# Gated mix of attention and a channel MLP: weight pieces split, statistics and first maxima moved, the tail's sums loaded in parts

## The chip, the cores and the metric

The kernel runs on one core of a Trainium2 chip. Five engines of the core matter here: TensorE (PE in the profile) multiplies matrices and writes PSUM banks of 128 x 512 float32, VectorE (DVE), ScalarE (ACT) and GpSimd (POOL) work elementwise, and SyncE (SP) issues most of the DMA transfers. Each engine takes its instructions in the order in which they were written and stands still at one whose semaphores are not there yet. The metric is the device time of one execution in microseconds, the median of three runs; the profile is of one more execution.

## The reference

The input x has 2048 tokens of width 576. What is computed:

```
g = sigmoid((x * gate_w).sum(-1, keepdims=True))
a = softmax_attention(x @ wqkv, 32 heads of 18) @ wo        # scale 18 ** -0.5
y = (x - mean(x)) / sqrt(var(x) + 1e-5)
b = gelu_tanh(y @ w1 + b1) @ w2 + b2                          # 576 -> 4608 -> 576
out = g * a + (1 - g) * b
```

Everything is float32. The kernel gets that precision out of TensorE by cutting each factor into a high part (a rounded copy, written by ScalarE) and a low part (the factor minus that copy, written by VectorE or GpSimd), and adding three products.

## The kernel before, in words

The work has three stages, and the order within each engine's queue is the order in which the Python code writes the instructions.

**Stage 1, the projections (to about 224 us of the span).** Four blocks `tb` of 512 tokens. For each block TensorE runs 17 groups `g` of 14 matmuls: nine `qk_group` (128 rows of Q and K, 512 tokens wide; L881 to L884) and eight `v_group` (128 tokens, 288 columns of V; L902 to L905), in PSUM banks of a pool of four, `ps_a`. Behind each group the code may hang other work, by tables at the head of the file:

- `W_AT`: before which groups of block 0 a piece of the QKV weights is cut into high and low (`split_w`, L751 on ScalarE, L752 on VectorE or GpSimd). The seven pieces arrive by DMA into two buffers of the pool `pp`, so a piece's load waits for the piece two before it. The bounds of the pieces are `W_CUT`.
- `N_AT`: behind which groups of block 0 its layer norm is worked out. `norm` has four stages: 0 and 1 take the statistics of two of the block's four groups of 128 tokens each (L844, L845) and stage 1 ends with the reciprocal deviation (L850 to L857); 2 and 3 take the gate's sum (L867) and, in block 0, write the normed tokens over x (L870). The gate's product goes to a scratch tile of the pool `pp`, too.
- `BLOCK[tb]`: the same for block `tb + 1`, whose x is loaded ahead (`load`). `stats` is the group behind which its statistics begin (stage 0, and stage 1 a group later), `rows` the group behind which they are transposed and stored (`stat_rows`, L826 to L828), `wide` the group behind which they are read back as rows spread over all partitions (`load_wide`, L832, into `wide`, which is the tile `qa` in the profile), `gate` the group behind which the gate's sums come, `x` the first of five groups behind which x is transposed (`x_chunk`, L757). `x_chunk` writes, from one bank: x minus the mean (L772, VectorE, needs `wide`), the high part (L774, ScalarE) and the low part (L775, VectorE). In block 0 `y_chunk` does the same with the normed tokens behind groups 12 to 16 (L757, L805, L806).
- `ROUNDS[tb](g)`: how many rounds of first maxima follow group `g`. A round is two score matmuls (L227) and two maxima over 512 scores on VectorE (L229, 128 x 512 to 128 x 1); its results give the softmax its first row maxima. Forty rounds must be done before stage 2.

**Stage 2, the loop (to about 2190 us).** 512 steps of attention, into which the MLP's matmuls are dealt out as filler, and in the last steps those of the tail's first blocks. The change does not touch its order.

**Stage 3, the tail.** `out_proj` runs four blocks `b` of 512 tokens. A block has eight groups of 14 matmuls (L1205), two for each 128 tokens; behind each, VectorE forms the result from the bank, the gate and the MLP's sums `BT[b][t]` (L1209). The banks are a pool of two, so a group waits for the result two groups before it. Between these results VectorE and ScalarE prepare the next block's factor: `normed(b, stage)` multiplies a 128 x 512 piece of the unscaled attention output `o` by the reciprocal sums `den` (L1122) and cuts it (L1125, L1132); `PLAN` sets behind which group which stage stands. The last unit of attention ends while block 1 is under way; then `over` loads what had to wait for it. `load_rest(b)` loads the last unit's rows of `o` and `den` (L1093, L1098), and `last_loads` the MLP sums of block 2 (`load_b`, L1104, tile `bt`), and `o` and `den` of block 3 (L1056, L1059, L1078, L1081). `load_den` calls `load_rest` at its end once the last unit is over.

DMA transfers take turns on eight completion counters, over all queues: an issue waits until the transfer eight places before it in the program has landed. SP's queue stands still for as long, with all that is behind it.

Of the kernel before, what the change touches and what calls it, by code (L numbers as in the profile page):

```python
# [8 lines left out]
F32 = mybir.dt.float32  # L9
F32R = mybir.dt.float32r  # L10
AF = mybir.ActivationFunctionType
ALU = mybir.AluOpType
# [4 lines left out]
P = 128  # L17
# [7 lines left out]
TB = 512  # L25
# [25 lines left out]
LAST = 28  # L51
PSTEP = (489, 492, 495, 497)
ORDER = (0, 1, 3, 2)
ROUNDS = [lambda g: 0, lambda g: 2 * (g in (9, 11, 13, 15)), lambda g: 2 * (g % 2 and g != 17),
          lambda g: 2 * (g in (4, 5, 6, 7, 8, 10, 12, 14))]
SLOTS = [lambda g: 0, lambda g: 0, lambda g: int(g >= 4), lambda g: 1 if g < 9 else 2]
SKIP = 0
N_AT = {3: (0, ()), 4: (1, ()), 7: (2, (0,)), 8: (3, (1,)), 9: (3, (2,)), 10: (3, (3,))}
BLOCK = [dict(stats=0, rows=4, wide=5, x=11, lag=4, gate=16, load=16),
         dict(stats=5, rows=8, wide=9, x=11, lag=3, gate=7, load=13),  # L60
         dict(stats=0, rows=3, wide=4, x=6, lag=3, gate=3)]
W_AT = {0: 1, 1: 2, 2: 3, 4: 4, 6: 5, 7: 6}
W_CUT = (0, 128, 416, 704, 992, 2 * D, 3 * D - 288, 3 * D)
# [5 lines left out]
def gated_mix_kernel(ctx: ExitStack, tc: tile.TileContext, x, wqkv, wo, w1, b1, w2, b2, gate_w, out):  # L69
    nc = tc.nc  # L70
    x = x[0]
# [15 lines left out]
    b_scr = dram.tile([S, D], F32, name="b_scr")  # L87
# [617 lines left out]
    with ExitStack() as a:  # L705
# [41 lines left out]
        def split_w(n, eng):  # L747
            c0 = W_CUT[n] if W_CUT[n] < 2 * D else W_CUT[n] - 2 * D
            hi, lo = [w_[:, :, c0:c0 + W_CUT[n + 1] - W_CUT[n]] for w_ in (W_QK if W_CUT[n] < 2 * D else W_V)]
            raw = wraw.pop(n)  # L750
            nc.scalar.activation(hi, raw, AF.Copy)  # L751
            eng.tensor_tensor(lo, raw, hi.bitcast(F32), op=ALU.subtract)  # L752

        def transposed(tb, c):
            ps = psum(ps_a)
# [182 lines left out]
        for tb in range(NB):  # L938
            work = [(qk_group, (tb, mt)) for mt in (range(9) if tb < 2 else (4, 0, 1, 2, 3, 5, 6, 7, 8))] + [(v_group, (tb, t, n)) for t in range(4) for n in range(2)]
            for g, (fn, args) in enumerate(work):  # L940
                if tb == 0:
                    if g in W_AT:
                        n = W_AT[g]
# [82 lines left out]
    def out_proj():  # L1026
# [36 lines left out]
        def load_den(b):  # L1063

            while len(stored) < (NU - 2 if b < 2 else NU - 1):
                run_due()
            if b == 0:
                wide = low.bitcast(F32)[:, 0:4, :]
                den = [low.bitcast(F32)[:, c, :] for c in range(5)]
            elif b % 2 == 0:  # L1070
                wide = KA[0].bitcast(F32).rearrange("p (c n) -> p c n", c=4)
                den = [wide[:, c, :] for c in range(4)] + [QA[2][:, :TB].bitcast(F32)]
            else:
                tile_ = io.tile([P, 5, TB], F32, name="den", bufs=1)
                wide = tile_[:, 0:4, :]
                den = [tile_[:, c, :] for c in range(5)]
            cols = slice(b * TB, (b + 1) * TB)
            nc.sync.dma_start(wide, ot_scr[1, 0:512, cols].rearrange("(c p) n -> p c n", p=P))  # L1078
            for h in range(2):
                e = 64 if b < 2 else LAST  # L1080
                nc.sync.dma_start(den[4][64 * h:64 * h + e], ot_scr[1, 512:512 + e, cols])  # L1081
            OT[b].append(den)
            if ended[0]:
                load_rest(b)

        ready = {0, 1}

# [10 lines left out]
                    nc.sync.dma_start(den[4][r:r + DH], sums[j:j + 1, :].to_broadcast([DH, TB]))  # L1098
            ready.add(b)

        def load_b(b):
            t0 = len(BT.setdefault(b, []))
            bt = io.tile([P, 4 - t0, D], F32, name="bt", bufs=2)
            nc.sync.dma_start(bt, b_scr[b * TB + t0 * P:(b + 1) * TB, :].rearrange("(t p) d -> p t d", p=P))  # L1104
            BT[b] += [bt[:, t] for t in range(4 - t0)]

        def load_b_first():
            BT[0] = [QA[0].bitcast(F32)[:, :D], VT[0].rearrange("p k e -> p (k e)")[:, :D]]
# [40 lines left out]
        held = []  # L1149

        def last_loads():
            load_b(2)
            load_o(3)
            load_den(3)
        waiting = []

        def go_on(last):
# [20 lines left out]
        io = ctx.enter_context(tc.tile_pool(name="c_io", bufs=3))  # L1178
        load_o(1)
        load_den(1)  # L1180
        load_b(0)
        yield 0
        for b in range(NB):
            if b == 1 and not ended[0]:
                held.append(last_loads)
            elif b == 1:
                last_loads()
            elif b + 1 < NB:
                load_b(b + 1)
            for t in range(4):  # L1190
                if b == 0 and t == 1:
                    load_o(2)
# [127 lines left out]
```

## Time and profile before

| | us |
| --- | --- |
| median of 3 runs | 2240.97 (2240.55 to 2241.92) |
| the profiled execution's own time | 2240.88 |
| its span | 2239.1 |
| TensorE busy | 2216.3 |
| VectorE busy | 1644.1 |
| ScalarE busy | 1427.3 |
| GpSimd busy | 1002.9 |

The profile counts time from the start of the span. A row of its timeline has the start, the time from the first start to the last end of the instructions merged in it, the engine, the line, the operation, what is written and read, the count, and in brackets the idle time before it and what ended it. A letter q behind an engine's name is its queue: there the time is that of issuing. A row of the waits has a sum, a count and the longest. Times of matmuls overlap, so the distance from one row's start to the next is what a stretch of matmuls takes.

### The profile page before, as it was taken

What the parts mean: (1) busy time and instruction counts of PE and PEld (TensorE: products, weight loads), DVE (VectorE), ACT (ScalarE), POOL (GpSimd) and SP (SyncE); (2) the same over time, 40 slices, a digit from 0 to 9 for tenths busy, and PEclk for the clock granted to TensorE, in tenths of its full rate; (3) what the DMA queues carried; (4) which work ended last, traced back from release to release, by engine and by line L of the source; (5) the groups of instructions that cost most, each with busy time, mean ns of one, the idle gap of its engine ahead of it and who ended that gap; (6) DMA issues with size and microseconds to landing.
All of it is one profiled execution on the core that took longest, in us unless ns stands there. A gap on an engine that the chain in (4) does not pass through costs nothing.

```text
span 2239.1 us, 51576 instructions
## 1 busy us (share of the span) xinstructions
PE 2216.3 (99%) x20528; PEld 1578.7 (71%) x20528; DVE 1644.1 (73%) x2886; ACT 1427.3 (64%) x2653; POOL 1002.9 (45%) x1001
## 2 busy tenths in 40 slices
PE   8999999999999999999999999999999999999999
PEld 7878666766767677667677667677676676676668
DVE  5685677777778777777777777777777777777734
ACT  4233677777767666666666666666666666666772
POOL 3241666666655444444454444444444444444710
PEclk9999999999999999999999999999999999999999
DMA  8767654445455524333354424233364323242264
GB/s 252 240 210 245 213 174 131 145 157 170 133 198 159 173 87 155 103 128 114 109 156 154 132 87 144 100 119 103 117 179 144 107 100 120 103 148 89 92 221 167
DMA packets 164104, 329.23 MB, mean 147 GB/s; under 512 B 56814, under 2 KB 84074, under 8 KB 153134
## 3 DMA queue, kind: packets, MB, share of 16 engines
q1 hardware_dynamic: 161766, 322.19, 44.3%
q8 instruction: 162, 2.65, 0.5%
q10 hardware_dynamic: 1968, 3.70, 0.4%
q14 instruction: 80, 0.66, 0.1%
q0 software_dynamic: 128, 0.03, 0.0%
HBM read 233.47 MB, written 96.17 MB: 147 GB/s over the span
## 4 chain that ended last, share of the span: by engine, by line
PE 91%; DVE 3%; DMA 2%; ACT 1%; issue 1%; POOL 1%; SPq 0%; DVEq 0%; ACTq 0%; POOLq 0%
PE ps L285 20%; PE ps L572 20%; PE ps L484 20%; PE ps L267 13%; PE ps L227 11%; PE ps L881 3%; PE ps L1205 2%; DVE m L229 1%; PE ps L902 1%; DMA qk_scr<-hl 1%; ACT zz L537 0%; DMA x<-in_B_w_dram 0%; PE ps L757 0%; DMA p<-in_A_wqkv_dram 0%; DVE hl L888 0%
## 5 line engine op out<-in xcount | busy, mean ns | idle before, releaser
L229 DVE TENSOR_REDUCE m<-ps 128x1 f32<-128x512 f32 x2048 | 1311.3, 683 | 408.8 <-PE ps L227 384.2
L270 ACT ACTIVATE p<-ps 128x512 f32<-128x512 f32 x1368 | 741.2, 596 | 381.8 <-PE ps L267 377.9
L484 PE MATMUL ps<-big,w 64*128 64x512 f32 x3708 | 567.3, 393 | 1.0 <-DVE z L504 0.6
L180 POOL TENSOR_SCALAR zz<-zz 128x512 f32<-128x512 f32 x288 | 178.3, 619 | 748.6 <-ACT zz L537 731.3
L270 ACT ACTIVATE ring<-ps 128x512 f32<-128x512 f32 x680 | 369.0, 596 | 189.1 <-PE ps L267 187.6
L572 PE MATMUL ps<-w,hh 64*128 64x288 f32 x4352 | 484.0, 294 | 1.9 <-DVE x L589 0.9
L267 PE MATMUL ps<-qa,ka 56*128 56x512 f32 x2048 | 459.3, 422 | 3.3 <-ACT p L270 1.8
L572 PEld LDWEIGHTS ps<-w,hh 64*128 64x128 f32 x4352 | 425.4, 186 | 29.3 <-DVE x L589 2.8
L227 PE MATMUL ps<-ka,qa 54*128 54x512 f32 x2048 | 435.1, 398 | 1.1
L484 PEld LDWEIGHTS ps<-big,w 64*128 64x128 f32 x3708 | 366.8, 186 | 68.9 <-DVE z L504 1.1
L180 POOL TENSOR_TENSOR zz<-zz,z 128x512 f32<-128x512 f32 x288 | 371.8, 1291 | 24.0
L267 PEld LDWEIGHTS ps<-qa,ka 56*128 56x128 f32 x2048 | 212.8, 184 | 221.4 <-DVE m L229 181.0
L572 PE MATMUL ps<-w,hl 64*128 64x288 f32 x2176 | 349.3, 292 | 0.8 <-POOL hl L180 0.8
L285 PE MATMUL ps<-p,vt 128*32 128x512 f32 x2560 | 322.8, 598 | 0.0
L227 PEld LDWEIGHTS ps<-ka,qa 54*128 54x128 f32 x2048 | 219.0, 184 | 27.6 <-DVE m L229 7.1
L572 PEld LDWEIGHTS ps<-w,hl 64*128 64x128 f32 x2176 | 232.2, 185 | 1.2 <-POOL hl L180 1.1
L180 POOL TENSOR_TENSOR hl<-zz,hh 128x512 fp32r<-128x512 f32 x136 | 176.7, 1299 | 11.4
L180 POOL TENSOR_TENSOR w<-x,w 128x576 fp32r<-128x576 f32 (+1 forms) x54 | 98.7, 1844 | 167.6 <-ACT w L392 134.3
L285 PE MATMUL ps<-ring,vt 128*32 128x512 f32 x1280 | 168.7, 598 | 0.0
L285 PEld LDWEIGHTS ps<-p,vt 128*32 128x32 f32 x2560 | 67.0, 109 | 142.7 <-issue 136.5
L589 DVE SCALAR_TENSOR_TENSOR x<-ps,x 128x288 f32<-128x288 f32 x256 | 103.8, 447 | 8.6 <-PE ps L572 8.4
L881 PE MATMUL ps<-big,wqk 128*128 128x512 f32 x432 | 108.7, 399 | 1.2 <-POOL wqk L752 0.7
(124 smaller groups left out, 1488.8 us busy)
## 6 DMA issues: line engine op xcount, KB each, us to landing
w<-w_scr SPq DMA_DIRECT2D x54, 1152.0 KB
w<-w_scr SPq DMA_DIRECT2D x108, 576.0 KB
x<-in_B_w_dram SPq DMA_DIRECT2D x72, 288.0 KB
w_scr<-w SPq DMA_DIRECT2D x18, 1152.0 KB
w_scr<-w SPq DMA_DIRECT2D x36, 576.0 KB
qa<-qk_scr SPq DMA_DIRECT2D x192, 72.0 KB
ka<-qk_scr SPq DMA_DIRECT2D x84, 144.0 KB
qk_scr<-hh SPq DMA_DIRECT2D x36, 256.0 KB
```

Source lines behind the costliest of these rows:

```text
L180: fn(*args, **kw)
L227: nc.tensor.matmul(ps, qa[r0:r0 + 54, t * P:(t + 1) * P], ka[r0:r0 + 54, kb * TB:(kb + 1) * TB], start=True, stop=True)
L229: nc.vector.tensor_reduce(M4[u][:, h, t, kb:kb + 1], ps, axis=AX.X, op=ALU.max)
L267: nc.tensor.matmul(ps[h], ka[r0:r0 + 56, kc * P:(kc + 1) * P], qa[r0:r0 + 56, qb * TB:(qb + 1) * TB], start=True, stop=True)
L270: nc.scalar.activation(RING[n % 3][:, qb, h], ps[h], AF.Exp, scale=SCALE)
L285: nc.tensor.matmul(OB[u][r:r + 32, :], v[:, k, 19 * h:19 * h + 32], RING[c % 3][:, qb, h, :], start=(k == 0), stop=(k == NT - 1))
L484: nc.tensor.matmul(ps[h], wt[w_][r, c, :], y[r, c, :], start=(k == 0), stop=(k == 26))
L572: mm = nc.tensor.matmul(ps[nn][:, :ND], h_[r, tok], w_[p_][r, cs[nn]], start=(k == 0), stop=(k == 6 * G - 1))
L589: nc.vector.scalar_tensor_tensor(dst, ps[nn][:, :ND], 0.5, b2b[:, cs[nn]] if g == 0 else dst, op0=ALU.mult, op1=ALU.add)
L881: nc.tensor.matmul(ps, w_[:, c, ms], big[:, s_, :], start=(k == 0), stop=False)
L902: nc.tensor.matmul(ps[:, :ND], big[:, s_, tok], w_[:, c, cs], start=(k == 0), stop=False)
L1205: nc.tensor.matmul(ps[:, :ND], OT[b][2][:, s_, tok], w_part(w_, c)[:, cs], start=(k == 0), stop=(k == 13))
```

## The change

The first two weight pieces are cut in two: rows 0 to 2 of the five row blocks first, then 3 and 4, each by its own ScalarE and VectorE instruction. The layer norm's stages 2 and 3 of block 0 stand behind groups 6, 7 and 8 where they stood behind 7 to 10, the statistics of block 1 begin a group later (their rows, too), those of block 2 a group earlier (and their rows and the gate's sums one and two groups earlier). The eight rounds of block 1 become six, behind groups 9, 10 and 16 where they stood behind 9, 11, 13 and 15; block 2 has two more, behind group 16. In the tail the MLP sums of block 2 are loaded in three transfers with `o` and `den` of block 3 between them, and `load_den` now calls `load_rest` ahead of its own loads.

```diff
-ROUNDS = [lambda g: 0, lambda g: 2 * (g in (9, 11, 13, 15)), lambda g: 2 * (g % 2 and g != 17),
+ROUNDS = [lambda g: 0, lambda g: 2 * (g in (9, 10, 16)), lambda g: 2 * (g % 2 or g == 16),
-N_AT = {3: (0, ()), 4: (1, ()), 7: (2, (0,)), 8: (3, (1,)), 9: (3, (2,)), 10: (3, (3,))}
+N_AT = {3: (0, ()), 4: (1, ()), 6: (2, (0, 1)), 7: (3, (2,)), 8: (3, (3,))}
...
-            nc.scalar.activation(hi, raw, AF.Copy)
-            eng.tensor_tensor(lo, raw, hi.bitcast(F32), op=ALU.subtract)
+            for cs in (slice(0, 3), slice(3, 5)) if n < 2 else (slice(0, 5),):
+                nc.scalar.activation(hi[:, cs], raw[:, cs], AF.Copy)
+                eng.tensor_tensor(lo[:, cs], raw[:, cs], hi[:, cs].bitcast(F32), op=ALU.subtract)
...
             cols = slice(b * TB, (b + 1) * TB)
+            OT[b].append(den)
+            if ended[0]:
+                load_rest(b)
             nc.sync.dma_start(wide, ot_scr[1, 0:512, cols].rearrange("(c p) n -> p c n", p=P))
...
-            OT[b].append(den)
-            if ended[0]:
-                load_rest(b)
...
-        def load_b(b):
+        def load_b(b, cuts=None):
...
-            nc.sync.dma_start(bt, b_scr[b * TB + t0 * P:(b + 1) * TB, :].rearrange("(t p) d -> p t d", p=P))
             BT[b] += [bt[:, t] for t in range(4 - t0)]
+            for c0, c1 in cuts or ((t0, 4),):
+                rows = b_scr[b * TB + c0 * P:b * TB + c1 * P, :]
+                nc.sync.dma_start(bt[:, c0 - t0:c1 - t0], rows.rearrange("(t p) d -> p t d", p=P))
+                yield
...
         def last_loads():
-            load_b(2)
+            parts = load_b(2, ((0, 1), (1, 2), (2, 4)))
+            next(parts)
             load_o(3)
+            next(parts)
             load_den(3)
+            next(parts)
```

VectorE's order in block 0, behind the low part of the seventh `qk_group` and to the first copy of V (`vt`) or just past it; `wv` is the last weight piece, `hl` a group's low part, `p,glog<-x,gwb` the gate's sum of 128 tokens, `x<-x,stats,rstd` their norming. Before:

```order
L752 TENSOR_TENSOR wv_128<-p,wv_127 128x5x288
L888 TENSOR_TENSOR hl<-ps,hh 128x512
L867 SCALAR_TENSOR_TENSOR p,glog<-x,gwb 128x576
L870 TENSOR_SCALAR x<-x,stats,rstd 128x640
L888 TENSOR_TENSOR hl<-ps,hh 128x512
L867 SCALAR_TENSOR_TENSOR p,glog<-x,gwb 128x576
L870 TENSOR_SCALAR x<-x,stats,rstd 128x640
L867 SCALAR_TENSOR_TENSOR p,glog<-x,gwb 128x576
L870 TENSOR_SCALAR x<-x,stats,rstd 128x640
L913 COPY vt_109<-ps 128x8x2x18
L867 SCALAR_TENSOR_TENSOR p,glog<-x,gwb 128x576
L870 TENSOR_SCALAR x<-x,stats,rstd 128x640
```

And now (lines after 751 have moved down by one):

```order
L868 SCALAR_TENSOR_TENSOR p,glog<-x,gwb 128x576
L871 TENSOR_SCALAR x<-x,stats,rstd 128x640
L868 SCALAR_TENSOR_TENSOR p,glog<-x,gwb 128x576
L871 TENSOR_SCALAR x<-x,stats,rstd 128x640
L753 TENSOR_TENSOR wv_128<-p,wv_127 128x5x288
L889 TENSOR_TENSOR hl<-ps,hh 128x512
L868 SCALAR_TENSOR_TENSOR p,glog<-x,gwb 128x576
L871 TENSOR_SCALAR x<-x,stats,rstd 128x640
L889 TENSOR_TENSOR hl<-ps,hh 128x512
L868 SCALAR_TENSOR_TENSOR p,glog<-x,gwb 128x576
L871 TENSOR_SCALAR x<-x,stats,rstd 128x640
L914 COPY vt_109<-ps 128x8x2x18
```

The first two of the four normings stand ahead of the last weight piece, and all four ahead of the first copy of V.

VectorE's order in block 1, from the maxima behind group 9 to the second-last input transpose; `m` is a round's maxima, `vt` a copy of V. Before:

```order
L229 TENSOR_REDUCE m_1036<-ps 128x1 x4
L913 COPY vt_109<-ps 128x8x2x18
L772 TENSOR_TENSOR p<-ps,qa_106 128x512
L775 TENSOR_TENSOR big<-ps,big 128x512
L229 TENSOR_REDUCE m_1036<-ps 128x1 x4
L913 COPY vt_110<-ps 128x8x2x18
L772 TENSOR_TENSOR p<-ps,qa_106 128x512
L775 TENSOR_TENSOR big<-ps,big 128x512
L772 TENSOR_TENSOR p<-ps,qa_106 128x512
L775 TENSOR_TENSOR big<-ps,big 128x512
L229 TENSOR_REDUCE m_1036<-ps 128x1 x4
```

And now:

```order
L229 TENSOR_REDUCE m_1040<-ps 128x1 x4
L914 COPY vt_109<-ps 128x8x2x18
L229 TENSOR_REDUCE m_1040<-ps 128x1 x4
L773 TENSOR_TENSOR p<-ps,qa_106 128x512
L776 TENSOR_TENSOR big<-ps,big 128x512
L914 COPY vt_110<-ps 128x8x2x18
L773 TENSOR_TENSOR p<-ps,qa_106 128x512
L776 TENSOR_TENSOR big<-ps,big 128x512
L773 TENSOR_TENSOR p<-ps,qa_106 128x512
L776 TENSOR_TENSOR big<-ps,big 128x512
L914 COPY vt_109<-ps 128x8x2x18
```

The maxima stand ahead of the input transposes' work instead of between it.

SP's order in the tail, behind `load_rest(2)`; `x` is `o` of block 3. Before:

```order
L1104 DMA bt<-b_scr 128x4x576
L1056 DMA x<-ot_scr 128x4x512
L1059 DMA x<-ot_scr 28x512 x2
L1078 DMA den<-ot_scr 128x4x512
L1081 DMA den<-ot_scr 28x512 x2
L1093 DMA x<-ot_scr 36x512 x2
L1098 DMA den<-dn_scr 18x512 x4
L1104 DMA bt<-b_scr 128x4x576
```

And now:

```order
L1108 DMA bt<-b_scr 128x576
L1057 DMA x<-ot_scr 128x4x512
L1060 DMA x<-ot_scr 28x512 x2
L1108 DMA bt<-b_scr 128x576
L1094 DMA x<-ot_scr 36x512 x2
L1099 DMA den<-dn_scr 18x512 x4
L1082 DMA den<-ot_scr 128x4x512
L1085 DMA den<-ot_scr 28x512 x2
L1108 DMA bt<-b_scr 128x2x576
L1108 DMA bt<-b_scr 128x4x576
```

The sums' second half (`128x2x576`) has moved behind `den`, and the last unit's six small loads ahead of it.

More of the change, by code (lines that the diff above doesn't have):

```diff
@@ L57 @@
 SKIP = 0
-N_AT = {3: (0, ()), 4: (1, ()), 7: (2, (0,)), 8: (3, (1,)), 9: (3, (2,)), 10: (3, (3,))}
-BLOCK = [dict(stats=0, rows=4, wide=5, x=11, lag=4, gate=16, load=16),
-         dict(stats=5, rows=8, wide=9, x=11, lag=3, gate=7, load=13),
+N_AT = {3: (0, ()), 4: (1, ()), 6: (2, (0, 1)), 7: (3, (2,)), 8: (3, (3,))}
+BLOCK = [dict(stats=1, rows=5, wide=6, x=11, lag=4, gate=16, load=16),
+         dict(stats=4, rows=7, wide=8, x=11, lag=3, gate=5, load=13),
          dict(stats=0, rows=3, wide=4, x=6, lag=3, gate=3)]
@@ L1180, in out_proj @@
         load_den(1)
-        load_b(0)
+        next(load_b(0))
         yield 0
```

2 lines of the change are left out of this document (1 added, 1 removed).

## The prediction

> **What bounds the kernel now.** I read the page's first part, then TensorE's waits, then the timelines of TensorE and of the engines it waits for, in the first 225 us and the last 90.
>
> ```profile
> span 2239.1 us, 51576 instructions
> PE 2216.3 (99%) x20528; PEld 1578.7 (71%) x20528; DVE 1644.1 (73%) x2886; ACT 1427.3 (64%) x2653; POOL 1002.9 (45%) x1001
> ```
>
> TensorE is busy for 99% of the span, and the change leaves its work as it is: forty rounds, the same groups. Only time in which TensorE stands, or runs at a lower clock, can go. The profiled execution took 2240.88 us, 1.78 over its span and 0.09 under the median 2240.97, so I subtract from the median.
>
> ```profile
> PE ps L757 <- DVE big L775: 1.4, 1, 1.4
> PE ps L1205 <- ACT big L1129: 1.3, 1, 1.3
> PE ps L902 <- DVE big L775: 1.3, 1, 1.3
> ```
>
> These three and smaller ones are where the edits point. But the waits count only idle time; the distances between starts show more.
>
> ```profile
> 9.01 3.46 PE L881 MATMUL ps<-big,wqk 128*128 128x512 f32 x12
> 13.79 2.60 PE L881 MATMUL ps<-big,wqk 128*128 128x512 f32 x10 [0.39 <-DVE wqk L752]
> 16.69 2.96 PE L881 MATMUL ps<-big,wqk 128*128 128x512 f32 x12
> 19.95 3.08 PE L881 MATMUL ps<-big,wqk 128*128 128x512 f32 x12
> 28.06 2.60 PE L881 MATMUL ps<-big,wqk 128*128 128x512 f32 x10 [0.72 <-POOL wqk L752]
> 40.76 1.76 PE L902 MATMUL ps<-wv,big 128*128 128x288 f32 x12
> 42.63 2.11 PE L902 MATMUL ps<-wv,big 128*128 128x288 f32 x12
> 51.93 2.48 PE L902 MATMUL ps<-wv,big 128*128 128x288 f32 x12 [1.27 <-DVE big L775]
> 54.68 1.80 PE L757 MATMUL ps<-ident,x 128*128 128x128 f32 x8
> 64.25 3.05 PE L881 MATMUL ps<-big,wqk 128*128 128x512 f32 x12
> 52.00:56.00 4.00, 4.00 (x21) 3.98 (x22) 2.03 (x4) 1.33 (x4) 1.28 (x1) 0.61 0.71 269
> ```
>
> A wide group goes by in 3.26 us (16.69 to 19.95), a V group in 1.87 (40.76 to 42.63). From 40.76 to block 1's first group at 64.25 stand eight V groups and ten transposes of some 0.35 us each: 18.5 us of work in 23.5. About 1.6 of the 5.0 lost is the clock: the last row, of four microseconds by windows, has 0.61 of full clock (third number from the end; behind it the DMA share and 269 GB/s).
>
> **The weight pieces.**
>
> ```profile
> 17.27 1.41 ACT L751 ACTIVATE wqk<-p 128x1440 fp32r<-128x1440 f32 x1 [3.71 <-DMA p<-in_A_wqkv_dram]
> 18.72 1.66 DVE L752 TENSOR_TENSOR wqk<-p,wqk 128x1440 fp32r<-128x1440 f32 x1 [2.37 <-ACT wqk L751]
> ```
>
> The third matmul of a group is the first that reads a low part. The first group lost some 0.3 us before it (12 matmuls in 3.46, against 2.96), the second 0.55. With three fifths of a piece cut first, about 1.0 us of VectorE in place of 1.66, both waits should go; the two further instructions on each engine cost about 0.2 us beside TensorE. But the third piece, not split, is set by its DMA: ScalarE starts at 17.27 when it lands, VectorE ends at 20.38, and TensorE's fourth group needs it at 19.95 + 2 x 0.23 = 20.4 already. What is won before is waited out here. I take 0; the bounds are 0 and 0.85 gained.
>
> **The statistics a group later.**
>
> ```profile
> 23.11 0.20 ACT L851 ACTIVATE sd<-var 128x4 f32<-128x4 f32 x1 [2.65 <-DVE var L850]
> 23.23 1.39 ACT L751 ACTIVATE wqk<-p 128x1440 fp32r<-128x1440 f32 x1
> 13.76 0.37 SPq L743 DMA_DIRECT2D p<-in_A_wqkv_dram  x1
> 34.28 3.30 POOL L752 TENSOR_TENSOR wv<-p,wv 128x1440 fp32r<-128x1440 f32 x1 [4.40 <-ACT wv L751]
> ```
>
> ScalarE's copy of the fourth piece stood behind the square root `sd`, which waits for VectorE. Now it stands ahead. It then starts when its piece lands. That was issued at 13.76, behind the third, and has 0.74 MB: at 269 GB/s 2.7 us after the third's 17.27, so about 20.0. With 1.4 for the copy and 3.3 for GpSimd the low part is there at 24.7. TensorE asks in its sixth group's third matmul, at 19.95 + 2 x 3.27 + 0.47 = 27.0. The stop at 28.06 goes: 1.0 us (0 if the piece lands over 2 us later). Next late is the chain of the second square root, for block 0: ScalarE's copy of the sixth piece, for GpSimd's step at 34.28, stands behind it. I estimate that this step moves to 34.8, one low part and the moved statistics being ahead of that root, and ends at 38.1.
>
> **The norming by groups.**
>
> ```profile
> 43.49 0.75 DVE L867 SCALAR_TENSOR_TENSOR p<-x,gwb 128x576 f32<-128x576 f32 x1
> 57.01 0.68 DVE L772 TENSOR_TENSOR p<-ps,qa 128x512 f32<-128x512 f32 x1
> 60.05 0.68 DVE L772 TENSOR_TENSOR p<-ps,qa 128x512 f32<-128x512 f32 x1
> ```
>
> Before, the normings ran from 43.49 on, four of 1.33 us with other work between, with TensorE's transposes on their heels. Now the first can start only when GpSimd has let go of the scratch tile, at 38.2 (the buffer that the sixth piece held). Two end at 40.9; the last weight piece behind them takes 1.66, to 42.5. The second V group asks for it at 41.8: a new wait of 0.75, in place of 0.35 before. The other two normings, with the groups' low parts between, end at 46.4. The first input transpose comes at 46.0, its L772 at 46.8. From there VectorE sets the pace: a chunk with both transposes takes it 2.6 to 3.04 us (57.01 to 60.05), TensorE 2.57. With four banks I get three short stops, 0.8 us together: 39.7 (40.76 less 1.0) + 18.5 + 0.75 + 0.8 = 59.75 for block 1's first group. Against 64.25 that is 4.5 for both edits, 3.5 of it here, the lost clock with it. If the clock falls all the same it is 1.9; without any stop, 5.0.
>
> A rule: the Trainium skill's page "TensorE: Matmul & The Clock Gate", Part 1, says that TensorE falls to half clock after an idle window of about 3.4 us, and Part 4 that transposes do not count as work. The trace agrees only with both: the clock fell behind the stop of 1.27 us at 51.93 and the eight transposes ahead of it, not behind 3.4 us of idle time. By that rule the new order, with under 1.2 us without an ordinary matmul, keeps the clock.
>
> **Block 1: rounds and the spread rows.**
>
> ```profile
> 96.35 0.56 SPq L828 DMA_DIRECT2D st_scr<-strow  x1
> 101.47 0.32 SPq L832 DMA_DIRECT2D qa<-st_scr  x1
> 105.15 0.69 DVE L772 TENSOR_TENSOR p<-ps,qa 128x512 f32<-128x512 f32 x1 [3.99 <-DMA qa<-st_scr]
> 107.34 0.63 PE L757 MATMUL ps<-ident,x 128*128 128x128 f32 x4 [1.43 <-DVE big L775]
> 107.90 2.23 PE L227 MATMUL ps<-ka,qa 54*128 54x512 f32 x4
> 114.85 1.94 PE L227 MATMUL ps<-ka,qa 54*128 54x512 f32 x4
> 170.51 0.73 PE L227 MATMUL ps<-ka,qa 54*128 54x512 f32 x4
> ```
>
> Two causes. TensorE's 1.43 us is a full set of banks, because VectorE waited 3.99 us for the spread rows: their store, issued at 96.35, had landed only at 101.47. Then two rounds waited for VectorE, whose maxima stood between the transposes' work (2.23 and 1.94 us against 0.73). The rounds behind 9 and 10 now end before the transposes, and three in place of four rounds save 0.75 more: 1.5 + 1.5 + 1.2 + 0.75 = 5.0, plus 0.3 of small delays. The spread rows must come some 1.5 us sooner relative to TensorE, though, for the third transpose asks earlier without a round before it. Their store is now issued one group's two stores (1.3 us) earlier and has 512 KB less in front of it, another 1.4 us at what the queues move; SP holds group 8's stores between. I get 103.2 to 103.7 on the old clock, where 103.6 is needed, and charge 0.3. I take 5.0; 3.0 if the rows come only 0.5 sooner, 5.6 at best.
>
> **Block 2** has a round more, 0.75 us, behind group 16, where it follows group 15's maxima at once: up to 0.5 of bank wait. I take 1.1 lost (0.75 to 2.0). Blocks 3 and the loop keep their order and their distances, 8 us earlier; no wait there is for a fixed time.
>
> **The tail.**
>
> ```profile
> 2196.49 0.39 SPq L1104 DMA_DIRECT2D bt<-b_scr  x1
> 2202.96 3.74 SPq L1081 DMA_DIRECT2D den<-ot_scr  x2
> 2211.55 0.69 DVE L1122 TENSOR_TENSOR x<-x,den 128x512 f32<-128x512 f32 x1 [1.63 <-DMA den<-ot_scr]
> 2213.18 0.51 DVE L1209 SCALAR_TENSOR_TENSOR res<-ps,gate,bt 128x288 f32<-128x288 f32 x1
> 2218.06 0.69 DVE L1122 TENSOR_TENSOR x<-x,den 128x512 f32<-128x512 f32 x1 [1.36 <-DMA den<-dn_scr]
> 2219.27 0.51 DVE L1209 SCALAR_TENSOR_TENSOR res<-ps,gate,bt 128x288 f32<-128x288 f32 x1
> 2219.93 1.57 PE L1205 MATMUL ps<-big 128*128 128x288 f32 x10 [1.28 <-ACT big L1129]
> DMA packets 2470, 4.91 MB, mean 317 GB/s; under 512 B 209, under 2 KB 209, under 8 KB 2468
> ```
>
> TensorE should have gone on at 2218.5; it waited until 2219.93 for the result at 2219.27 (the row names ScalarE, but a group's first matmul waits for its bank), which stood behind the small loads `dn_scr`. Those now land some 8 us sooner: 1.4 to gain. What is late next: the sums' second half, needed at 2213.1, is now behind `den`, and its issue waits for the counter of an output store that ScalarE issues at about 2208. All that is moved ahead of its end, 4.98 MB at the 317 GB/s of the last row (2197.5 to 2213), takes 15.7 us: it lands at 2213.3 at best, with SP's stops (as at 2202.96) about 2214.5. From that result to the one that frees TensorE's bank VectorE needs 5.0 us: 2219.6, gain 0.3; at 2215.7 it is 0.9 lost. `den`, too, comes no sooner. I take 0 (1.4 gained to 1.3 lost).
>
> A rule against the split: the skill's "DMA: Bandwidth & Descriptors", Anatomy of one DMA, puts a fixed cost of some 2.0 us on each transfer, which two more transfers would make 4.0. No row here shows that cost alone. By it the sum would be 3.6 us worse.
>
> **Sum:** 0 + 1.0 + 3.5 + 5.0 - 1.1 + 0 = 8.4 gained: 2240.97 - 8.4 = 2232.6, say 2232.5.
>
> **Rivals.** (1) The spread rows come late: DMA transfers of block 1 keep their time while TensorE is 4.5 us ahead. For it speaks the wait of 3.99 us; against it that the issues follow TensorE's groups. The rows then come at 103.5 where TensorE needs them at 103.6 - 4.5 = 99.1: 4.4 us of wait, and block 1 gives 0.9: 2236.7. (2) The clock falls again or elsewhere, 1.6 us: 2234.1. (3) Each further transfer costs SP a stop like the one inside the row at 2202.96, which has two issues in 3.74 us and so stood some 3.1: 6.2 for two, of which I have counted 1.2, and 5.0 more at the sums put TensorE 4.6 later: 2237.1. Against it: SP stood there for a counter, and most issues did not. The skill's fixed cost, above, has the same sign. (4) The earlier loop waits for its first weights and keys at its old time: 2241. No row shows such a wait before. (5) Slower: the sums' second half, held by the counter of that output store. Each microsecond after 2214.9 costs one; to be 4.5 us slower than before it would have to land at about 2228, 13 late.
>
> **How the numbers follow.** Forecast 0.66, (1) 0.13, (2) 0.07, (3) 0.05, (4) 0.06, (5) 0.03. A measurement tells 0.2% (4.5 us) from no change; (1) lies about at that bound and is halved. Faster 0.66 + 0.07 + 0.06 = 0.79, same 0.07 + 0.05 + 0.06 = 0.18, slower 0.03. The bounds of the terms give 2228 to 2239; 8 in 10 lie in 2229.5 to 2237.0.
>
> **What would show it.** In the new profile: no wait for GpSimd's weights near 27 and a new one near 20; block 1's first wide group at about 59.7; no row under full clock at 50; rounds of 0.73 in block 1 and its end at about 109; the loop's start some 8 us earlier; in the tail VectorE's wait at the sums, not at `dn_scr`. I am wrong if the first 110 us give under 5.

## The result, and the profile after

The changed kernel took 2235.98 us (median; 2235.26 to 2236.66), the kernel before in the same comparison 2240.72: ratio 0.998, 95% interval 0.9971 to 0.9989. It is 4.7 us faster where 8.4 were forecast, and inside the range. Beside three of the experiments it ran again, at 0.9984 (0.9975 to 0.9993).

The first line of the changed kernel's page:

```profile
span 2234.4 us, 51590 instructions
```

Its timeline over the first 217 us, TensorE's with a row of VectorE's (a row of four L227 matmuls is two rounds):

```profile
20.76 2.59 PE L882 MATMUL ps<-big,wqk 128*128 128x512 f32 x10 [0.80 <-DVE wqk L753]
40.72 1.65 DVE L753 TENSOR_TENSOR wv<-p,wv 128x1440 fp32r<-128x1440 f32 x1
60.40 3.05 PE L882 MATMUL ps<-big,wqk 128*128 128x512 f32 x12
94.66 0.86 PE L227 MATMUL ps<-ka,qa 54*128 54x512 f32 x4
108.97 0.73 PE L227 MATMUL ps<-ka,qa 54*128 54x512 f32 x4
109.63 3.06 PE L882 MATMUL ps<-big,wqk 128*128 128x512 f32 x12
216.40 0.50 PE L267 MATMUL ps<-qa,ka 56*128 56x512 f32 x2
```

The same row of the kernel before:

```profile
224.39 0.50 PE L267 MATMUL ps<-qa,ka 56*128 56x512 f32 x2
```

So the loop starts 8.0 us sooner. Block 1 starts at 60.40 instead of 64.25 (3.85 won), block 2 at 109.63 instead of 118.67 (another 5.19), and blocks 2 and 3 give 1.05 back. From the loop's start to the end of the span the kernel before took 2239.1 - 224.39 = 2014.7 us, the changed one 2018.0: **3.3 us are lost in the tail**, and 8.0 - 3.3 = 4.7. The tail of the changed kernel, by the timelines of SP's queue, VectorE and TensorE:

```profile
2193.06 0.75 SPq L1060 DMA_DIRECT2D x<-ot_scr  x2
2198.11 3.14 SPq L1099 DMA_DIRECT2D den<-dn_scr  x4
2201.30 0.39 SPq L1082 DMA_DIRECT2D den<-ot_scr  x1
...
2207.35 0.69 DVE L1126 TENSOR_TENSOR x<-x,den 128x512 f32<-128x512 f32 x1 [5.15 <-DMA den<-ot_scr]
2209.88 0.52 DVE L1216 SCALAR_TENSOR_TENSOR res<-ps,gate,bt 128x288 f32<-128x288 f32 x1 [0.81 <-DMA bt<-b_scr]
...
2208.53 2.77 PE L1212 MATMUL ps<-big 128*128 128x288 f32 x10 [3.17 <-DVE res L1216]
```

and four microseconds of it by windows (the third number from the end is TensorE's clock):

```profile
2207.00:2211.00 4.00, 2.47 (x10) 2.47 (x11) 2.84 (x6) 1.26 (x2) 0.00 (x0) 0.62 1.04 380
```

The first load of `den` in the kernel before, and SP's three longest waits for landings ahead of the last load there:

```profile
2199.47 0.46 SPq L1078 DMA_DIRECT2D den<-ot_scr  x1
SPq L1093 <- DMA out_dram<-res: 3.9, 1, 3.9
SPq L1081 <- DMA out_dram<-res: 3.1, 1, 3.1
SPq L1081 <- DMA bt<-b_scr: 3.0, 1, 3.0
```

`den` is issued at 2201.30, 1984.9 us behind the loop's start; before it was 1975.1 us (at 2199.47), so it now comes 9.8 us later. VectorE stands 5.15 us for it, TensorE 3.17, and within that stop the clock falls (0.62). What SP waited for there, in the changed kernel:

```profile
SPq L1099 <- DMA x<-ot_scr: 3.0, 2, 2.8
SPq L1060 <- DMA out_dram<-res: 2.4, 1, 2.4
SPq L1099 <- DMA out_dram<-res: 1.7, 1, 1.7
```

Loads of `o` and of the small rows wait for output stores of ScalarE's queue, and the small rows for an earlier load of `o`, with none of which they share data. In the built program the transfers of both queues use eight completion counters in turn, so that an issue waits until the transfer eight places ahead of it has landed. Three such waits now stand ahead of `den`: 2.4 us for a store, 2.8 for the load of `o` and 1.7 for the next store, 6.9 of the 9.8 us. The rest is mostly the issuing of the transfers that were moved ahead. Before, the first load of `den` was issued ahead of all three long waits (they stand at L1081 and L1093, behind L1078).

### The profile page after: what moved, and what is told of

Read it like the earlier page. It is cut to its first block, busy times and chain, and to the rows that moved or that the text cites. A ratio compares the mean times of both kernels' runs of the same rounds, so it can differ in the third digit from the quotient of the medians.

```text
span 2234.4 us, 51590 instructions
## 1 busy us (share of the span) xinstructions
PE 2214.2 (99%) x20528; PEld 1580.9 (71%) x20528; DVE 1645.2 (74%) x2888; ACT 1427.1 (64%) x2655; POOL 1003.2 (45%) x1001
## 4 chain that ended last, share of the span: by engine, by line
PE 92%; DVE 3%; DMA 2%; ACT 1%; issue 1%; POOL 1%; SPq 0%; ACTq 0%; DVEq 0%; POOLq 0%
PE ps L285 20%; PE ps L572 20%; PE ps L484 20%; PE ps L267 13%; PE ps L227 11%; PE ps L882 3%; PE ps L1212 2%; PE ps L903 2%; DVE m L229 1%; DMA x<-in_B_w_dram 1%; ACT zz L537 0%; POOL w L180 0%; PE ps L758 0%; DMA p<-in_A_wqkv_dram 0%; PE ps L885 0%
## 5 line engine op out<-in xcount | busy, mean ns | idle before, releaser
L227 PE MATMUL ps<-ka,qa 54*128 54x512 f32 x2048 | 433.5, 398 | 0.6
L227 PEld LDWEIGHTS ps<-ka,qa 54*128 54x128 f32 x2048 | 218.8, 185 | 25.2 <-DVE m L229 4.5
```

Source lines behind the costliest of these rows:

```text
L227: nc.tensor.matmul(ps, qa[r0:r0 + 54, t * P:(t + 1) * P], ka[r0:r0 + 54, kb * TB:(kb + 1) * TB], start=True, stop=True)
```

## The experiments

All places from the profiled executions; "to the end" is the span less the loop's start. The ratios are to the kernel before in the same comparison (e1 to e4 in one, e5 to e8 in the second, the rest in the third; the kernel before had medians of 2238.63, 2239.76 and 2240.31 there, so single times of different comparisons are not to be set against each other).

| run | block 1 | block 2 | loop | to the end | median | ratio (95%) |
|---|---|---|---|---|---|---|
| before | 64.25 | 118.67 | 224.39 | 2014.7 | 2240.72 | 1 |
| changed | 60.40 | 109.63 | 216.40 | 2018.0 | 2235.98 | 0.998 (0.9971-0.9989) |
| changed, again | 60.40 | 109.61 | 216.41 | 2017.5 | 2237.50 | 0.9984 (0.9975-0.9993) |
| e1 tail back | 60.41 | 110.17 | 216.96 | 2014.9 | 2233.44 | 0.997 (0.9958-0.9981) |
| e2 tail only | 63.68 | 118.62 | 224.30 | 2019.7 | 2242.88 | 1.0014 (1.0005-1.0023) |
| e3 small loads back | 60.40 | 109.64 | 216.41 | 2020.8 | 2237.26 | 0.9993 (0.9984-1.0002) |
| e4 sums whole | 60.71 | 109.97 | 216.72 | 2019.5 | 2236.84 | 0.9987 (0.9978-0.9996) |
| e5 rounds back | 60.25 | 112.82 | 218.53 | 2014.0 | 2234.25 | 0.9971 (0.996-0.9982) |
| e6 no split | 60.34 | 109.56 | 216.31 | 2014.1 | 2231.61 | 0.9961 (0.9946-0.9976) |
| e7 norming back | 60.41 | 110.07 | 216.86 | 2014.2 | 2232.68 | 0.9966 (0.9953-0.9979) |
| e8 block 1's rows back | 60.40 | 113.09 | 219.84 | 2014.6 | 2234.35 | 0.9975 (0.9964-0.9985) |
| e9 block 0's statistics back | 62.53 | 111.78 | 218.53 | 2014.4 | 2234.32 | 0.9968 (0.9955-0.9981) |
| e10 two small loads | 60.68 | 109.92 | 216.70 | 2014.6 | 2234.42 | 0.9969 (0.9956-0.9981) |
| e11 two stores short | 60.65 | 110.36 | 217.10 | 2021.0 | 2239.24 | 0.9994 (0.9985-1.0003) |

**The tail.** First it was put back in the changed kernel (e1), and put alone into the kernel before (e2).

```diff
...
 def last_loads():
-    parts = load_b(2, ((0, 1), (1, 2), (2, 4)))
-    next(parts)
+    load_b(2)
     load_o(3)
-    next(parts)
     load_den(3)
-    next(parts)
...
 def load_den(b):
...
-    OT[b].append(den)
-    if ended[0]:
-        load_rest(b)
     nc.sync.dma_start(wide, ot_scr[1, 0:512, cols].rearrange("(c p) n -> p c n", p=P))
...
+    OT[b].append(den)
+    if ended[0]:
+        load_rest(b)
```

(`load_b` goes back with it: one load, no `yield`.) e2 has the same lines the other way round, in the kernel before.

> The changed kernel with only its tail put back: the sums of the last block in one load, the small loads behind the wide loads of den. Theory (the tail's edit costs what stage 1 gains too much): 2232.7 us, 3.2 less than the changed kernel's 2235.98; the loop still starts at 216.4; no stop at the result L1216 of over 1.5 us and no half clock in the last 30 us; dn_scr is again what VectorE waits for. Rival (the clock has to fall once, wherever; the tail only happened to take it): half clock is found at another place and the time stays at 2235.5 to 2236.5. Rival (an earlier end of the rounds costs the tail, whatever its order of loads): 2236, with the stop at L1216 still there.

> The kernel before with only the tail's edit. Theory: stage 1 as before (loop at 224.4, half clock near 53 us), den issued some 9 us later than before, a stop of about 3.2 us at L1216's result and half clock behind it: 2243.5 to 2244, 3.2 slower than before's 2240.7. Rival (the clock falls once at most): 2242 to 2242.5, no half clock in the tail. Rival (the loss needs the earlier rounds of the changed kernel): 2240.7, no stop in the tail over 1.5 us.

VectorE and TensorE in the tail of e1:

```profile
2204.91 0.69 DVE L1123 TENSOR_TENSOR x<-x,den 128x512 f32<-128x512 f32 x1 [1.73 <-DMA den<-ot_scr]
2210.92 0.69 DVE L1123 TENSOR_TENSOR x<-x,den 128x512 f32<-128x512 f32 x1 [0.94 <-DMA den<-dn_scr]
2212.79 1.57 PE L1206 MATMUL ps<-big 128*128 128x288 f32 x10 [0.85 <-ACT big L1130]
```

and of e2, with a stop of its block 0 and the clock there:

```profile
52.61 1.84 PE L902 MATMUL ps<-wv,big 128*128 128x288 f32 x12 [1.28 <-DVE big L775]
52.00:56.00 4.00, 3.39 (x27) 3.42 (x28) 2.89 (x6) 1.82 (x5) 1.88 (x2) 1.00 0.69 264
...
2215.55 0.69 DVE L1125 TENSOR_TENSOR x<-x,den 128x512 f32<-128x512 f32 x1 [4.70 <-DMA den<-ot_scr]
2216.72 2.77 PE L1211 MATMUL ps<-big 128*128 128x288 f32 x10 [2.71 <-DVE res L1215]
```

The tail's edit alone makes the kernel before slower (4.25 us by the medians; 5.0 by "to the end", in a profiled execution that was the longest of its eleven and whose clock stays at half for about 6.8 us in the tail, against 3.4 in the changed kernel). Without it the changed kernel needs 2014.9 us behind the loop's start, as before. The loss does not hang on the earlier rounds. In e1 the clock is whole in the first 224 us and from 2195 to 2227: it need not fall somewhere. The theory stands for the tail. Its time for e1 was 2232.7, measured 2233.44; the intervals of e1 and of the changed kernel overlap, so the 3.1 us between them behind the loop's start rest on the traces and on e2. One expectation for e2 failed: half clock near 53 us. Block 0 is that of the kernel before, with the same stop (1.28 us at 52.61, 1.27 before), and the clock is whole there (1.00 from 52 to 56); it fell in block 1 instead (0.57 from 110 to 114).

Then one of the two edits at a time:

e3 is the changed kernel with the second half of e1's diff:

```diff
 def load_den(b):
...
-    OT[b].append(den)
-    if ended[0]:
-        load_rest(b)
     nc.sync.dma_start(wide, ot_scr[1, 0:512, cols].rearrange("(c p) n -> p c n", p=P))
...
+    OT[b].append(den)
+    if ended[0]:
+        load_rest(b)
```

> The changed kernel with the small loads (last rows of o, and dn_scr) put back behind the wide loads of den, the sums still loaded in three parts. Theory A (the small loads ahead of den delay it): den is issued about 5 us sooner than in the changed kernel, the stop at L1216 falls from 3.2 us to under 1.5, no half clock in the tail: 2232.5 to 2233.5. Theory B (the two further transfers for the sums delay den, by a landing counter each): den comes as late as in the changed kernel, 2235.5 to 2236.5.

and e4 with the first:

```diff
...
 def last_loads():
-    parts = load_b(2, ((0, 1), (1, 2), (2, 4)))
-    next(parts)
+    load_b(2)
     load_o(3)
-    next(parts)
     load_den(3)
-    next(parts)
```

> The changed kernel with the sums of the last block in one load ahead of o, the small loads still ahead of the wide loads of den. Theory A (the small loads delay den): den still late, stop at L1216 of 2.5 us or more: 2235 to 2236.5. Theory B (the split sums delay it): 2232.5 to 2233.5 and no half clock in the tail. If both delay it by about half, this and the run with the small loads put back both lie near 2234.

SP, VectorE and TensorE in the tail of e3:

```profile
2195.18 0.67 SPq L1079 DMA_DIRECT2D den<-ot_scr  x1
2202.07 5.12 SPq L1099 DMA_DIRECT2D den<-dn_scr  x4
...
2205.11 0.69 DVE L1126 TENSOR_TENSOR x<-x,den 128x512 f32<-128x512 f32 x1 [1.72 <-DMA den<-ot_scr]
2211.86 0.52 DVE L1216 SCALAR_TENSOR_TENSOR res<-ps,gate,bt 128x288 f32<-128x288 f32 x1 [5.02 <-DMA bt<-b_scr]
...
2212.43 2.77 PE L1212 MATMUL ps<-big 128*128 128x288 f32 x10 [4.01 <-DVE res L1216]
```

and of e4:

```profile
2201.89 0.38 SPq L1082 DMA_DIRECT2D den<-ot_scr  x1
2208.86 0.69 DVE L1123 TENSOR_TENSOR x<-x,den 128x512 f32<-128x512 f32 x1 [6.15 <-DMA den<-ot_scr]
2210.04 1.99 PE L1206 MATMUL ps<-big 128*128 128x288 f32 x10 [4.16 <-DVE res L1210]
```

Theory A is right about `den`. With the small loads back (e3) it is issued 1978.8 us behind the loop's start, 6.1 sooner than in the changed kernel, and VectorE's wait for it falls to 1.72; with the sums whole (e4) it is issued 1985.2 us behind, as late as in the changed kernel, and the wait is 6.15. Against the kernel before, the split of the sums alone delays `den` by 3.7 us, the small loads alone by 10.1, both together by 9.8. But neither theory foresaw the time of e3, 2237.26: with `den` nearly in time, the sums' second half is late in its place, behind the small loads' stop (5.02). e4's 2236.84 is a little above theory A's range. Each edit alone has a longer stop of TensorE (4.01 and 4.16) than both together (3.17), and its profiled execution loses more (6.1 and 4.8 us to the end, against 3.3). That the timed runs differ so is not shown: the intervals of the three ratios overlap, and part of e3's loss is the clock, which stays at half for about 6.8 us there.

Two experiments on what SP stands for. e10 is the changed kernel with the tail back and the weight pieces uncut, and halves the number of the small `dn_scr` loads at the same bytes:

```diff
-    for j in range(2):
-        r = 64 * h + LAST + j * DH
-        nc.sync.dma_start(den[4][r:r + DH], sums[j:j + 1, :].to_broadcast([DH, TB]))
+    r = 64 * h + LAST
+    nc.sync.dma_start(den[4][r:r + 2 * DH], sums.unsqueeze(1).to_broadcast([2, DH, TB]))
```

> The changed kernel with its tail as before, without the cut of the weight pieces, and with each pair of small loads dn_scr joined into one (two transfers in place of four, the same bytes). Theory (each transfer takes a counter, and SP stands for the counters): the wait of 0.9 us at dn_scr and TensorE's stop of 0.5 to 0.9 behind it go, 2231.0 to 2231.6, 4.5 us under the changed kernel in the same comparison. Rival (the stops follow the bytes, not the number of transfers): the stop stays, 2231.6 to 2232.5.

e11 is the changed kernel, and lets two output stores land early without a change in the count or order of the transfers; it leaves 127 of their 128 rows unwritten. The changed kernel itself ran beside both.

```diff
-    nc.scalar.dma_start(out[tt * P:(tt + 1) * P, :], res)
+    rows = 1 if tt in (5, 7) else P
+    nc.scalar.dma_start(out[tt * P:tt * P + rows, :], res[:rows])
```

> The changed kernel with two of ScalarE's output stores in the tail cut to one row of 128 (their other rows of the output are not written); every transfer keeps its place and its counter. Theory (SP stands until those stores have landed, before it can issue den): den's first load is issued 3 us or more before 2201.3, TensorE's stop of 3.2 us falls under 1, no half clock: 2232.5 to 2233.5. Rival (den comes late by the bytes ahead of it): the two stores are 0.59 MB, 1.6 us at 370 GB/s, so den's issue at 2199.7 or later, a stop of 1.6 us or more: 2234.3 or more.

> The changed kernel once more, beside the three below, for their comparison. The loop at 216.4 to 217, a stop of about 3 us at L1216's result behind the loads of den, half clock after it, 2235 to 2237 us.

Of this, the loop's start and the stop came (216.41, 3.03 us), the half clock did not; the median, 2237.50, is above the range.

The tail of e10, SP's queue and TensorE:

```profile
2191.03 5.79 SPq L1060 DMA_DIRECT2D x<-ot_scr  x2
...
2206.74 1.60 PE L1205 MATMUL ps<-big 128*128 128x288 f32 x10 [1.28 <-DVE res L1209]
```

SP's longest wait in the tail of e11:

```profile
SPq L1108 <- DMA out_dram<-res: 5.1, 1, 5.1
```

and its timeline, SP's queue and TensorE:

```profile
2200.55 0.39 SPq L1082 DMA_DIRECT2D den<-ot_scr  x1
2207.01 1.21 SPq L1108 DMA_DIRECT2D bt<-b_scr  x2
...
2207.25 1.60 PE L1212 MATMUL ps<-big 128*128 128x288 f32 x10 [0.80 <-DVE res L1216]
```

In e10 four transfers fewer gained nothing (2014.6 to the end; e6, the same kernel with all of them, 2014.1): other transfers now follow the output stores' counters, and SP stands at `o` instead. Its waits for landings from 2185 us to the last load sum to 11.6 us, against 11.3 in e6. The theory, that fewer transfers mean fewer stops, falls. Nor is its rival shown, since the stop moved. The median, 2234.42, lies above both ranges.

In e11 `den` came sooner: 1.9 us by the loop's start (2200.55 against 2201.76 in the changed kernel beside it, with the loop 0.7 later), where 3 were expected, and TensorE's stop for it fell from 3.0 to 0.80. That the stores' landing holds `den` is borne out. That the gain is smaller than expected has a reason in the rows: even a store of one row released SP only 2.4 us behind its issue (2190.32 to 2192.75), where the whole one took 3.8 in the changed kernel (2189.24 to 2193.06). The time is not borne out: the next store, queued behind the earlier `den`, landed late, and the sums' second half stood 5.1 us for it. This is the mechanism of the prediction's rival (5). 2239.24 lies where the rival put it, "2234.3 or more", but the stop is not for `den`.

**The first 225 us.** Five runs that all have the tail of e1, so that only these places differ. e6 drops the cut of the first weight pieces:

```diff
-    for cs in (slice(0, 3), slice(3, 5)) if n < 2 else (slice(0, 5),):
+    for cs in (slice(0, 5),):
```

> The changed kernel with its tail as before and without the cut of the first two weight pieces. Theory (what the cut wins is waited out at the third piece): the first wide group takes 3.46 again, the second waits 0.4, the third piece's wait near 20 falls from 0.8 to 0.3 or less, and the loop starts within 0.3 us of 216.7: no change in time. Rival (the cut is worth its full 0.85): every later group, and the loop, 0.8 to 0.9 later.

TensorE in e6:

```profile
13.96 2.60 PE L882 MATMUL ps<-big,wqk 128*128 128x512 f32 x10 [0.54 <-DVE wqk L753]
20.12 3.18 PE L882 MATMUL ps<-big,wqk 128*128 128x512 f32 x12
```

The two early waits are back (the first wide group takes 3.46 again, an undisturbed one 2.96, and the second waits 0.54), the one at the third piece shrinks (3.18), and block 1 starts at 60.34: the cut is worth nothing, as the theory had it, within the 0.5 us by which runs with the same block 0 differ (e10, too, is uncut and has 60.68).

e7 puts back the norming's groups:

```diff
-N_AT = {3: (0, ()), 4: (1, ()), 6: (2, (0, 1)), 7: (3, (2,)), 8: (3, (3,))}
+N_AT = {3: (0, ()), 4: (1, ()), 7: (2, (0,)), 8: (3, (1,)), 9: (3, (2,)), 10: (3, (3,))}
```

> The changed kernel with its tail as before and the norming of block 0 in the groups of the kernel before. Theory: a V group waits over 1 us for VectorE near 50, half clock near 52, block 1 starts 3.5 later than 60.4, at 63.9, the loop at 220.2, 3.5 slower. Without half clock 1.9: block 1 at 62.3, the loop at 218.6. Rival (the norming was not what TensorE waited for, the statistics a group later gave all of it): block 1 at 60.4 to 60.8, no change in time.

and e9 block 0's statistics of the next block:

```diff
-BLOCK = [dict(stats=1, rows=5, wide=6, x=11, lag=4, gate=16, load=16),
+BLOCK = [dict(stats=0, rows=4, wide=5, x=11, lag=4, gate=16, load=16),
```

> The changed kernel with its tail as before and the statistics in block 0 back in the groups of the kernel before; the norming stays moved. The run with the norming alone put back lost nothing, so: theory A (ScalarE's second square root, not the norming's place, held the last weight piece, and that the normings): the wait for GpSimd near 28 returns, the last weight piece is at VectorE past 40.5 again, a V group waits over 0.5 us, block 1 starts at 61.9 to 64.3, the loop at 218.2 or later. Theory B (either move is enough to clear the normings, and this one loses only the stop near 28): block 1 at 61.0 to 61.6, the loop at 217 to 217.8, 1 us slower.

VectorE in e7, the last weight piece and the first norming, and TensorE's largest stop between the first V group and block 1:

```profile
38.73 1.66 DVE L753 TENSOR_TENSOR wv<-p,wv 128x1440 fp32r<-128x1440 f32 x1 [2.85 <-ACT wv L752]
...
40.91 0.75 DVE L868 SCALAR_TENSOR_TENSOR p<-x,gwb 128x576 f32<-128x576 f32 x1
...
49.35 1.85 PE L903 MATMUL ps<-wv,big 128*128 128x288 f32 x12 [0.32 <-DVE big L776]
```

and in e9 the last weight piece on VectorE and TensorE's stops:

```profile
41.29 1.66 DVE L753 TENSOR_TENSOR wv<-p,wv 128x1440 fp32r<-128x1440 f32 x1 [0.67 <-ACT wv L752]
...
28.32 2.59 PE L882 MATMUL ps<-big,wqk 128*128 128x512 f32 x10 [0.73 <-POOL wqk L753]
54.22 1.85 PE L903 MATMUL ps<-wv,big 128*128 128x288 f32 x12 [1.49 <-ACT v L912]
```

For e7 the rival was right, not the theory: it loses nothing, 60.41 again. Moving the statistics (and with them ScalarE's square root, behind the fourth weight piece's copy) brings the last weight piece to VectorE at 38.73 instead of 41.31, and the normings behind it start at 40.91 where the kernel before has 43.49. The chain can be followed in e7: ScalarE copies the fourth piece at 19.80 (23.23 before), GpSimd ends its low part at 24.6 (28.0), and with the scratch buffer free the next pieces' loads are issued at 24.63 (28.03) and, for the last one, 29.42 (32.12). That alone ends the pile-up. e9 is theory A on every number: the stop for GpSimd is back, the piece is late, a V group waits 1.49, block 1 starts at 62.53. So of the 3.85 us the statistics give all. The norming alone gives 1.7 (64.25 to 62.53), part of which is the clock: against e2, whose block 0 is the old one at full clock, it is 1.2 (63.68). On top of the statistics it gives nothing.

e5 has the rounds of blocks 1 and 2 where they were before:

```diff
-ROUNDS = [lambda g: 0, lambda g: 2 * (g in (9, 10, 16)), lambda g: 2 * (g % 2 or g == 16),
+ROUNDS = [lambda g: 0, lambda g: 2 * (g in (9, 11, 13, 15)), lambda g: 2 * (g % 2 and g != 17),
```

> The changed kernel with its tail as before (so that only the first 225 us differ from it) and the rounds of blocks 1 and 2 where the kernel before has them; the spread rows stay a group earlier. Beside the same kernel with the new rounds: block 2 starts at 109.9, the loop at 216.7, about 2233. Theory (the rounds behind the transposes wait for maxima): two rounds of about 2 us again and one round more, block 2 starts at 113.3 (1.5 + 1.2 + 0.75 later), the loop at 219.3 since block 2 has a round less: 2.5 us slower than with the new rounds. Rival (the spread rows alone made the gain): block 2 starts at 110.6, the loop at 216.5, no change in time.

and e8 the row of block 1:

```diff
-         dict(stats=4, rows=7, wide=8, x=11, lag=3, gate=5, load=13),
+         dict(stats=5, rows=8, wide=9, x=11, lag=3, gate=7, load=13),
```

> The changed kernel with its tail as before and block 1's statistics and spread rows a group later, as in the kernel before; the new rounds stay. Theory (the spread rows must come earlier for the new rounds to pay): VectorE waits 3.5 to 4 us for them, TensorE stops 1.5 to 3 us at a bank, block 2 starts at 111.4 to 113. Rival (with the new rounds the rows' place does not matter): a wait of 1 to 2 us on VectorE, no stop of TensorE, block 2 at 109.6 to 110.2 and the loop at 216.4 to 217.

Block 1 in e5, rounds and VectorE's wait for the spread rows:

```profile
99.29 0.69 DVE L773 TENSOR_TENSOR p<-ps,qa 128x512 f32<-128x512 f32 x1 [4.10 <-DMA qa<-st_scr]
...
102.26 2.02 PE L227 MATMUL ps<-ka,qa 54*128 54x512 f32 x4
109.00 1.94 PE L227 MATMUL ps<-ka,qa 54*128 54x512 f32 x4
```

and in e8, VectorE's gate sums and the rounds that wait for maxima:

```profile
92.97 0.76 DVE L868 SCALAR_TENSOR_TENSOR p<-x,gwb 128x576 f32<-128x576 f32 x1
93.77 0.76 DVE L868 SCALAR_TENSOR_TENSOR p<-x,gwb 128x576 f32<-128x576 f32 x1
...
95.20 2.52 PE L227 MATMUL ps<-ka,qa 54*128 54x512 f32 x4 [0.47 <-DVE m L229]
...
101.57 0.69 DVE L773 TENSOR_TENSOR p<-ps,qa 128x512 f32<-128x512 f32 x1 [1.88 <-PE ps L758]
```

e5 follows the theory: two rows of four score matmuls take about 2 us each, block 2 starts at 112.82 (113.3 expected), and blocks 2 and 3 take 1.1 less than with the new rounds. The loop starts 1.6 us later than in e1, where 2.5 were expected. VectorE waits as long for the spread rows as before (4.10, and 3.99), yet TensorE does not stop at a bank: the rows come 1.9 us sooner, counted from block 1's start.

e8 lies in the range of its theory (113.09) by a mechanism that was not named: VectorE has no wait for the spread rows there (the 1.88 is for TensorE). The row of the table also moves the gate's sums (`gate`); a group later, two of them (1.5 us) stand ahead of the maxima, the four score matmuls at 95.20 take 2.52 instead of 0.86, and half clock follows (0.50 at 98 to 100). This is read from the trace; no run moved `gate` alone. Block 1 takes 52.57 us in e5 and 52.69 in e8 (the half clock in it), against 54.42 before and 49.23 in the changed kernel (49.2 to 49.8 in the runs with its block 1): each move alone gives about 1.8, both together 5.19.

## Why the prediction was right or wrong

The direction was right, and the first 110 us gave 9.0 us (9.5 in the working). The time lies inside the range, but the step on the tail does not hold, and its loss lies outside that step's own bounds. The range covered it because it also had room for misses that did not come; that part is luck. 2235.98 is nearer to the rivals (1) and (3), 2236.7 and 2237.1, than to the forecast.

- **The weight pieces**: 0, and 0 (e6), with the wait at the third piece where it was put (0.80 at 20.76). The first group's loss was read as 0.3; its rows, 3.46 against 2.96, say 0.5.
- **Statistics and norming**: 4.5 forecast, 3.85 measured; block 1 at 59.75 against 60.40. The timeline of VectorE was right to 0.2 us (the first norming started at 38.06, the last weight piece ended at 42.37), and no row under full clock stands there. But the split into 1.0 and 3.5 was wrong: the 3.5 was put down to the norming, and e7 shows that it belongs to the statistics. The step's second half, the weight piece landing 2.6 us sooner, had been worked out only as far as GpSimd. Nor was the clock worth 1.6 of the 3.5: from the stop's end to block 1's start the kernel before takes 12.32 us, e2 with the same stop at full clock 11.07, so it was 1.25. And the same stop behind the same eight transposes (2.8 us without an ordinary matmul in both) left e2's clock whole: that the two together make the clock fall, as the prediction read its trace, does not hold.
- **Block 1**: 5.0 forecast, 5.19. The spread rows still kept VectorE waiting (1.01 us at 98.74), but not TensorE; that the new rounds needed the gate's sums out of the way (e8's trace) was not in the working.
- **Blocks 2 and 3**: 1.1 forecast, 1.05.
- **The tail**: 0 taken, between 1.4 gained and 1.3 lost; 3.3 lost in the profiled execution, 2.8 in the other. This is the step that failed, and it holds 3.3 of the 3.7 us between forecast and result. It watched the sums' second half and passed over `den` with "`den`, too, comes no sooner", at no price. In fact `den` is issued 9.8 us later by the loop's start: the transfers moved ahead of it brought three waits for counters, 6.9 us together, and VectorE stood 5.15 us for it. The late sums were there too, at 0.81. "VectorE's wait at the sums, not at `dn_scr`" came half true: the wait at `dn_scr` went, one at `den` took its place.
- **The rivals**: (1) and (4) did not happen. (2), "the clock falls again or elsewhere", did, in the tail, but as a sequel of the stop for `den`. (3) had SP's stops as the danger, which is right, but put them at the sums, and priced them by the number of transfers: e4, with no transfer added, loses 4.8, and e10, with four fewer than e6, gains none. What counts in these traces is whose landing an issue waits for. The Trainium skill's page "DMA: Bandwidth & Descriptors", Anatomy of one DMA, gives a fixed cost of about 2.0 us to each transfer on GpSimd's path (these are SP's), and the loss of 3.3 looks like the 3.6 worked out from it; the two runs disagree with that reading. (5) came as far as the 0.81 at the sums, and in full in e11.

The lowest ratio measured is e6's, the changed kernel with the tail as before and the weights uncut: 0.9961 (0.9946 to 0.9976). The runs do not tell it from the others with that tail (0.9966 to 0.9975), and its interval overlaps the changed kernel's, which begins at 0.9971; that the old tail is the better one rests on the time behind the loop's start, 2.5 us or more shorter in every one of them.

## What to carry to other kernels

When loads are reordered on a queue whose counters are reused, write the waits of that queue into the working: for each moved transfer, which earlier transfer (of any queue that shares the counters) must land before it may be issued, and which load then stands behind it. When several edits clear one pile-up, put each back alone: here either of two moves looked like the cause, one of them was worth nothing beside the other, and one row of a table moved a second thing that mattered. A gain ahead of the loop went through to the end in full; what was lost was lost by the edit at the end.

## What the runs showed of the hardware

A stop does not decide by its length whether TensorE's clock falls. In the profiled execution of the changed kernel it falls 2.6 us into a stop of 3.17 us (0.50 from 2208 on); in the other, at the same place, a stop of 3.03 us leaves it whole (1.00 from 2199 to 2219):

```profile
2208.73 1.60 PE L1212 MATMUL ps<-big 128*128 128x288 f32 x10 [3.03 <-DVE res L1216]
```

In e2 it falls 2.0 us into a stop of 2.71 us (0.51 from 2216 on), and the stop of 1.28 us in its block 0 leaves it whole, where the kernel before had half clock. The Trainium skill's page "TensorE: Matmul & The Clock Gate", Part 1, says that the activity window of 3413 ns runs free of the kernel's start. These runs agree with that: half clock lasts about 3.4 us in the kernel before and in the changed one, about 6.8 in the tails of e2 and e3, and one and the same stop falls on either side. The page also puts the fall behind a whole idle window, which e2's 2.0 us do not bear out.

Of the 1.7 us that 3.4 us at half clock would cost, an estimate, the two profiled executions of the changed kernel show 0.5 behind the loop's start (2018.0 and 2017.5). The timed executions of the changed kernel, run again, go with the clock: four with a mean clock of 1.000 took 2235.06 to 2236.47 us, four with 0.998 took 2237.66 to 2240.01, and the three between them 2235.71 to 2237.52.

From the issue of an output store of ScalarE to the time when SP could go on took 3.8 us in the changed kernel (2189.24 to 2193.06), 5.5 in e11 for one issued behind `den` (2201.47 to 2207.01), about 7.2 in e10 (2189.34 to 2196.5), and 2.4 for a store of one row (e11). What sets it between 2.4 and 7.2 no run here shows.
